# A chunked state-space scan feeding a bilinear feed-forward: from four-block waves to a hand-ordered pipeline over blocks of 128 tokens

## The chip, the cores and the metric

One core of one Trainium2 chip. The metric is the device time of one execution in microseconds (us). TensorE, the matrix engine, appears as PE in the profile and its weight loads as PEld; VectorE is DVE, ScalarE is ACT, GpSimd is POOL, and SyncE, which here only issues transfers, is SP. PSUM is the accumulator memory that TensorE writes and DVE and ACT read; both kernels lay it out in banks of 512 float32 per partition. A matmul can be given a strip of 32 rows of TensorE's 128x128 array (row-tiled), of 32 columns (column-tiled), or of both; `tile_position` names the strip, and the profile prints its shape with a star, as `32*128`, `128*32` or `32*32`. The rest use the whole array (`128*128`).

A run more than 1.5% above the fastest of its kernel counts as slow and is left out of every ratio here; medians are of all runs.

## The reference

```python
# x: (4, 8, 768, 32)   a: (4, 8, 768)   B, C: (4, 8, 768, 16);   chunk = 32
for c in range(nc):
    ...
    cum = np.cumsum(la, axis=-1)                              # la = log a
    L = np.exp(cum[:, :, :, None] - cum[:, :, None, :]) * causal
    M = np.einsum('bhin,bhjn->bhij', Cc, Bc) * L
    y_intra = np.einsum('bhij,bhjd->bhid', M, xc)
    y_inter = np.einsum('bhin,bhnd->bhid', Cc, state) * np.exp(cum)[..., None]
    y[:, :, sl] = y_intra + y_inter
    state = decay_full[..., None, None] * state + np.sum(Bx, axis=2)
x = y.transpose(0, 2, 1, 3).reshape(3072, 256)
out = (x @ w_a) * (x @ w_b) @ w_out                           # 256 -> 1536 -> 256
```

Both kernels take chunks of 128 tokens instead of 32, which gives the same result: 6 blocks for each of 4 sequences, so 24 blocks, each with 8 heads of 32 channels and 16 states. The scan of a sequence is serial from block to block; the feed-forward of a block needs only that block's scan.

## The kernel before

The feed-forward works on groups of 512 tokens, four blocks. A group is put into a list of pieces when its four blocks have been scanned, and three pieces follow each later scan. The framework's scheduler may reorder what is written here.

```python
for b in range(nb):
    for blk in range(NBLK):
        emit_scaling(b, blk)                       # six DVE operations: BCm, Bd, Cd, CmE, CmO, X16
        ...
        # five transposes on TensorE: BCm, CmE, CmO, Cd, and Cd shifted by one head
        # scores: four row-tiled matmuls; mask by four DVE operations
        for u in range(2):
            for hh in range(4):                    # y_intra, column-tiled
                nc.tensor.matmul(py[32*g : 32*g+32, 0:128], X16[:, 32*h : 32*h+32], T1r[...], ...,
                                 tile_position=(0, 32 * g))
            for hh in range(4):                    # y_inter, one 16-row tile for each head
                nc.tensor.matmul(py[32*g : 32*g+32, 0:128], states16[blk][32*m : 32*m+16, ...], rhs_ci, ...,
                                 tile_position=(32 * m, 32 * g))
        ...
        if (_gb + 1) % 4 == 0 and ...:
            ffn_enqueue((_gb + 1) // 4 - 1)
        ffn_emit(3)
```

The feed-forward's matmuls stream 512 columns each; the output has one accumulator (`bufs=1`), so each of the four output groups of 128 tokens waits until the one before it has been copied out.

```python
for f in range(2):
    nc.tensor.matmul(a_ps, Wa[:, f, k*128 : (k+1)*128], X2T[:, f, j*NTOKT : (j+1)*NTOKT], ...)
...
nc.scalar.activation(out=a_sb, in_=a_ps, func=AF.Identity, scale=HSCALE)
nc.vector.scalar_tensor_tensor(out=hk, in0=b_ps, scalar=1.0, op0=ALU.mult, in1=a_sb, op1=ALU.mult)
...
pFO = ctx.enter_context(tc.tile_pool(name="pFO", bufs=1, space=bass.MemoryType.PSUM))
```

The head loads eight constants before the decays `a`, then takes their log and three cumulative sums for each of the six blocks, with three different triangular matrices (18 float32 matmuls).

## Time and profile before

| | before |
|---|---|
| time, median of 3 runs | 203.91 us (203.80 to 205.24) |
| span of the profiled run | 203.1 us |
| busy share PE, DVE, ACT, POOL | 87%, 56%, 44%, 11% |
| first feed-forward matmul | 41.88 us |
| last projection ends | near 192.4 us |

Three stretches are worth separating: up to the first feed-forward matmul, from there to the end of the last projection, and the rest. This is the view of the kernel before by stretch. Its columns are the stretch, its length, TensorE's busy time (and instructions), the granted clock, the share of the DMA engines, and GB/s.

```profile
0.00:41.88 41.88, 24.39 (x178) 1.00 1.01 137
41.88:192.40 150.52, 145.96 (x1200) 0.98 0.25 42
192.40:203.10 10.70, 5.48 (x44) 0.98 0.14 49
```

In the long middle stretch TensorE is idle for only 150.5 - 146.0 = 4.6 us. More speed there has to come from less TensorE work; the first and last stretch have waits to remove. Two rows of the table of groups show work that the change takes away or moves: the y_inter matmuls with 16 rows, and the scaling's cast of x, which leaves DVE. The columns are the shapes, the count, then busy us and the mean ns of one.

```profile
L400 PE MATMUL pyy<-BCT,st 16*32 16x128 f16 x96 | 11.9, 236 | 0.0
...
L225 DVE CAST x_all<-xf_all 128x256 f16<-128x256 f32 x24 | 7.0, 294 | 16.3 <-DMA xf_all<-in_x_dram 16.3
```

### The profile page before, as it was taken

The numbers are of one execution on the slowest core, as the hardware profiler recorded it, in microseconds if no ns is written. First come the engines' busy times: TensorE is split into PE (matmuls) and PEld (weight loads), VectorE is DVE, ScalarE is ACT, GpSimd is POOL, SyncE is SP. The second block draws the span as 40 slices with busy tenths as digits, with TensorE's granted clock in tenths as the row PEclk, the third lists the DMA queues.
The fourth block names the chain that finished last, engine by engine and source line by source line (L and its number), as shares of the span: only waits on it lengthen the run. The fifth ranks groups of instructions, "written<-read, shape, count | busy, mean of one in ns | idle before, by whom it ended". The sixth has DMA issues, their size and how long they took to land.

```text
span 203.1 us, 3886 instructions
## 1 busy us (share of the span) xinstructions
PE 175.8 (87%) x1418; PEld 94.5 (47%) x1418; DVE 113.4 (56%) x320; ACT 88.7 (44%) x226; POOL 21.9 (11%) x79
## 2 busy tenths in 40 slices
PE   0007989999999999999999998999989999899962
PEld 0007864433446444465434564344744346534442
DVE  6002148668897869988486422866225673236710
ACT  2013033535653456634456424565436564435511
POOL 5000202211011110011100111101111011100000
PEclk9999999999999889999999999999999999969999
DMA  5999998998899860001000010000110000200011
GB/s 75 211 222 159 113 112 98 110 111 106 104 114 127 102 129 31 0 26 60 21 0 0 17 65 31 2 0 3 52 52 3 0 0 29 77 0 2 3 52 52
DMA packets 81363, 12.53 MB, mean 62 GB/s; under 512 B 75648, under 2 KB 80800, under 8 KB 81344
## 3 DMA queue, kind: packets, MB, share of 16 engines
q1 hardware_dynamic: 79248, 9.93, 32.6%
q0 software_dynamic: 2096, 2.36, 7.2%
q8 instruction: 11, 0.18, 0.4%
q14 instruction: 8, 0.07, 0.1%
HBM read 11.50 MB, written 3.15 MB: 72 GB/s over the span
## 4 chain that ended last, share of the span: by engine, by line
PE 75%; ACT 7%; SPq 5%; DMA 4%; DVE 4%; issue 3%; ACTq 0%
PE a_ps L255 18%; PE o_ps L284 16%; PE b_ps L264 15%; PE pyy L381 8%; PE pa_m L357 6%; DMA xf_all<-in_x_dram 4%; PE pyy L400 4%; SPq L234 2%; ACT a_sb L273 2%; ACT o_sb L293 2%; DVE t1u L367 2%; PE pd L169 2%; PE q0a L329 2%; PE q1a L341 1%; PE pcum L169 1%
## 5 line engine op out<-in xcount | busy, mean ns | idle before, releaser
L275 DVE SCALAR_TENSOR_TENSOR hk<-b_ps,a_sb 128x512 f16<-128x512 f32 x72 | 49.8, 691 | 30.7 <-ACT a_sb L273 23.4
L273 ACT ACTIVATE a_sb<-a_ps 128x512 f32<-128x512 f32 x72 | 42.8, 599 | 26.1 <-PE a_ps L255 23.8
L367 DVE TENSOR_TENSOR t1u<-pa_m,caus_sb 128x256 f16<-128x256 f32 x96 | 35.7, 417 | 27.3 <-PE pa_m L357 27.1
L255 PE MATMUL a_ps<-x2t,Wa 128*128 128x512 f16 x144 | 47.3, 396 | 0.7 <-DVE hk L275 0.3
L264 PE MATMUL b_ps<-x2t,Wb 128*128 128x512 f16 x144 | 45.8, 393 | 0.0
L284 PE MATMUL o_ps<-Wo,hk 128*128 128x256 f16 x288 | 40.4, 273 | 2.1 <-ACT o_sb L293 1.5
L284 PEld LDWEIGHTS <-hk 128*128 128x128 f16 x288 | 26.0, 97 | 10.0 <-issue 3.2
L413 ACT CAST x2t<-pyy 128x128 f16<-128x128 f32 x48 | 12.7, 266 | 35.6 <-PE pyy L400 34.7
L381 PE MATMUL pyy<-t1u,x_all 128*32 128x128 f16 x192 | 21.7, 238 | 1.7 <-DVE t1u L367 0.4
L429 POOL TENSOR_TENSOR st<-st,CdBS 128x64 f32<-128x64 f32 x24 | 7.3, 304 | 135.5 <-ACT CdBS L351 135.5
L264 PEld LDWEIGHTS <-Wb 128*128 128x128 f16 x144 | 13.4, 98 | 16.0 <-issue 1.9
L381 PEld LDWEIGHTS <-x_all 128*32 128x32 f16 x192 | 9.6, 94 | 21.4 <-issue 17.5
L255 PEld LDWEIGHTS <-Wa 128*128 128x128 f16 x144 | 13.0, 100 | 14.0 <-issue 6.5
L357 PE MATMUL pa_m<-BCT 32*128 32x256 f16 x96 | 16.6, 294 | 2.7 <-ACT BCT L334 2.4
L293 ACT ACTIVATE o_sb<-o_ps 128x256 f32<-128x256 f32 x24 | 9.2, 383 | 21.4 <-PE o_ps L284 18.5
L225 DVE CAST x_all<-xf_all 128x256 f16<-128x256 f32 x24 | 7.0, 294 | 16.3 <-DMA xf_all<-in_x_dram 16.3
L132 PE MATMUL p_lat<-ident,la 32*128 32x32 f32 x12 | 2.8, 398 | 15.0 <-ACT la L128 15.0
L334 ACT CAST BCT<-q0a 128x384 f16<-128x384 f32 x24 | 11.5, 478 | 4.9 <-PE q0a L332 4.7
L400 PE MATMUL pyy<-BCT,st 16*32 16x128 f16 x96 | 11.9, 236 | 0.0
L400 PE MATMUL pyy<-CdBS,st 16*32 16x128 f16 x96 | 11.6, 235 | 0.0
L357 PEld LDWEIGHTS <-BCT 32*128 32x128 f16 x96 | 5.2, 92 | 10.1 <-issue 4.4
L132 PEld LDWEIGHTS p_lat<-ident,la 32*128 32x128 f32 x12 | 2.6, 324 | 15.0 <-ACT la L128 15.0
(53 smaller groups left out, 147.6 us busy)
## 6 DMA issues: line engine op xcount, KB each, us to landing
xf_all<-in_x_dram SPq DMA_DIRECT2D x24, 128.0 KB, 3.3
out_dram<-o_sb SPq DMA_DIRECT2D x24, 128.0 KB, 1.7
bn_all<-in_B_dram SPq DMA_DIRECT2D x24, 64.0 KB, 3.1
cn_all<-in_C_dram SPq DMA_DIRECT2D x24, 64.0 KB, 3.0
Wa<-in_moe_w_a_dram POOLq DMA_DIRECT2D x1, 768.0 KB, 7.3
Wb<-in_moe_w_b_dram POOLq DMA_DIRECT2D x1, 768.0 KB, 10.8
Wo<-in_moe_w_out_dram POOLq DMA_DIRECT2D x1, 768.0 KB, 14.9
p_sb<-p SPq DMA_DIRECT2D x2, 64.0 KB, 8.1
```

The source lines that it names most:

```text
L255: nc.tensor.matmul(a_ps, Wa[:, f, k * 128 : (k + 1) * 128], X2T[:, f, j * NTOKT : (j + 1) * NTOKT], start=(f == 0), stop=(f == 1), skip_gr ...
L264: nc.tensor.matmul(b_ps, Wb[:, f, k * 128 : (k + 1) * 128], X2T[:, f, j * NTOKT : (j + 1) * NTOKT], start=(f == 0), stop=(f == 1), skip_gr ...
L273: nc.scalar.activation(out=a_sb, in_=a_ps, func=AF.Identity, scale=HSCALE)
L275: nc.vector.scalar_tensor_tensor(out=hk, in0=b_ps, scalar=1.0, op0=ALU.mult, in1=a_sb, op1=ALU.mult)
L284: nc.tensor.matmul(o_ps, hks[k][:, st * 128 : (st + 1) * 128], Wo[:, k, :], start=(k == 0), stop=(k == NK - 1), skip_group_check=True,)
L293: nc.scalar.activation(out=o_sb, in_=o_ps, func=AF.Identity, scale=1.0 / HSCALE)
L334: nc.scalar.copy(BCT[:, 0:384], q0a[:, 0:384])
L357: nc.tensor.matmul(pa_m, BCT[32 * m : 32 * m + 32, 0:128], BCT[32 * m : 32 * m + 32, 128:384], start=True, stop=True, skip_group_check=Tru ...
L367: nc.vector.tensor_tensor(out=T1s[m // 2][:, (m % 2) * 256 : (m % 2) * 256 + 256], in0=pa_tiles[m], in1=caus_sb[:, 0:256], op=ALU.mult,)
L381: nc.tensor.matmul(py[32 * g : 32 * g + 32, 0:128], X16[:, 32 * h : 32 * h + 32], T1r[:, hh * 128 : hh * 128 + 128], start=True, stop=Fals ...
L400: nc.tensor.matmul(py[32 * g : 32 * g + 32, 0:128], states16[blk][32 * m : 32 * m + 16, (b * 2 + par) * 32 : (b * 2 + par) * 32 + 32,], rh ...
L413: nc.scalar.copy(X2T[:, u, b * S + blk * 128 : b * S + blk * 128 + 128], pys[u][:, 0:128],)
```

## The change

The intent is to feed TensorE without gaps from early on:

1. **Order by hand.** The scheduler is switched off. Turn t holds the scan of block t, the projections of block t-1, and the output of block t-2.
2. **Blocks of 128 tokens in the feed-forward too**, four 128-column products side by side in one PSUM bank, so it starts after the first block and not after four.
3. **Mid-block decay factors.** One pair of factors, exp(+c) for C and exp(-c) for B, with c counted from the middle of the block, serves scores, y_inter and the carry. The state is carried as it stands at the middle of the next block; a single factor `G` for each block and head takes it from middle to middle.
4. **Block-diagonal state.** The eight 16x32 states are spread into one 128x256 matrix with zeros elsewhere, so y_inter is two full matmuls and not eight small ones.
5. **PSUM.** Transposes, scan output, carry and scores share one tile `SC` of four banks; four further banks rotate for the feed-forward.
6. **Head.** The decays are loaded first, the weights come in seven pieces, TensorE runs 40 dummy matmuls, and the scaling moves from DVE to POOL.

The core of the diff, with cuts:

```diff
-    NTOKT = 512
-    ident = const.tile([128, 128], f16)
-    nc.sync.dma_start(ident, id128_t.ap())
-    ...                                              # seven more constants, then a
+    nc.sync.dma_start(a_sb, a.rearrange("b h s -> (b h) s"))
+    nc.scalar.dma_start(c32, p32_t.ap())
+    nc.scalar.dma_start(c16, p16_t.ap())
+    ...
+    psf = ctx.enter_context(tc.tile_pool(name="psf", bufs=4, space=PSUM))
+    SC = ps4.tile([128, 4, 512], f32, name="SC")
+    TT = SC[:, 0, :].bitcast(f16)
+    PY = SC[:, 1, :]
+    DS = SC[:, 2, :]
+    M3 = SC[:, 3, :]
+    ctx.enter_context(tc.manual_schedule())
+    ...
+    nc.tensor.matmul(cums, P63, laT, ...)            # one cumulative sum from mid-block, all blocks
+    nc.scalar.activation(out=fB, in_=cums, func=AF.Exp, scale=-1.0)
+    nc.scalar.activation(out=fC, in_=cums, func=AF.Exp)
+    ...
+    def pv(t):
+        if blk > 0:
+            for u in range(2):
+                nc.tensor.matmul(PY[:, u*128 : u*128+128], s["Sbd"][:, u*128 : u*128+128], s["BCT"][:, 256:384], ...)
+        ...                                          # y_intra into PY, carry into DS, both column-tiled
+        nc.scalar.activation(out=X2T[:, t], in_=PY[:, 0:256]..., func=AF.Copy, scale=YS / XS)
+        nc.vector.scalar_tensor_tensor(out=U32[:, b, blk + 1, :], in0=DS[:, 0:D], scalar=g, op0=ALU.mult,
+                                       in1=gU[:, b, blk, :], op1=ALU.add)
+        nc.gpsimd.tensor_tensor(out=Sbd..., in0=U32[:, b, blk + 1, :]...broadcast..., in1=maskbd..., op=ALU.mult)
+    ...
-            ffn_emit(3)
-    ffn_emit(1000)
+    for t in range(NT + 2):
+        scores(t); mask(t, 0)                        # (abridged)
+        scale(t + 1, ...); load(t + 3)
+        ffn_unit(t - 1, 0); mask(t, 1)
+        ffn_unit(t - 1, 1); ffn_unit(t - 1, 2)
+        pv(t)
+        transposes(t + 1)
+        ffn_out(t - 2)
```

## The prediction

> **What bounds the kernel now.** I read the page first, for who is busy and when.
>
> ```profile
> PE 175.8 (87%) x1418; PEld 94.5 (47%) x1418; DVE 113.4 (56%) x320; ACT 88.7 (44%) x226; POOL 21.9 (11%) x79
> ...
> PE   0007989999999999999999998999989999899962
> ...
> PEclk9999999999999889999999999999999999969999
> DMA  5999998998899860001000010000110000200011
> ```
>
> TensorE is full from slice 4 to 38 (a slice is 5.08 us); DVE and ACT have half the span free, and DMA, full for the first third, is idle after it. So there are three parts: a head without matmuls, a long body bound by TensorE, a short tail. The chain that ended last, in order of time, gives their limits:
>
> ```profile
> 10.58 8.52 DMA xf_all<-in_x_dram
> ...
> 29.89 0.44 PE pa_m L357 x2
> 33.25 0.80 PE pa_m L357 x4
> 36.54 0.80 PE pa_m L357 x4
> 39.83 0.80 PE pa_m L357 x4
> 41.95 0.52 PE a_ps L255
> ...
> 95.93 0.67 PE pa_m L357 x4
> ...
> 122.76 0.67 PE pa_m L357 x4
> ...
> 149.95 0.67 PE pa_m L357 x4
> ```
>
> Head: four blocks are scanned alone, 3.3 us each, and only at 41.95 does the feed-forward begin. Body: the same four-block pattern returns after 26.83 and 27.19 us, so 6.75 us a block. The tail I read in the timeline: the last feed-forward ends near 192.5, four output groups follow one by one at 2 us (one accumulator), and the span ends at 203.1.
>
> Next, in the timeline of TensorE, what one matmul really costs, because a busy TensorE is not one at its peak: I read the spacing of starts.
>
> ```profile
> 35.16 0.31 PE L330 MATMUL q0a<-ident,cme 128*128 128x128 f16 x1
> 35.27 0.31 PE L331 MATMUL q0a<-ident,cmo 128*128 128x128 f16 x1
> ...
> 94.92 0.22 PE L330 MATMUL q0a<-ident,cme 128*128 128x128 f16 x1
> 94.98 0.22 PE L331 MATMUL q0a<-ident,cmo 128*128 128x128 f16 x1
> 95.04 0.22 PE L332 MATMUL q0a<-ident,cd_all 128*128 128x128 f16 x1
> 95.09 0.22 PE L337 MATMUL q1a<-ident,cd_all 128*128 128x128 f16 x1
> ```
>
> The same 128-column matmul, each with its own weight load, is 110 ns from the next at 35 us and 55 ns at 95 us. The clock was half until about 45 us, which the page's clock row (9 there) does not show. Twelve 256-column output matmuls take 1.47 us, so 109 ns each; two 512-column ones 0.43 us, 215 each. Useful floor per block at full clock: 12 x 0.215 (288 / 24 matmuls) = 2.6 for the two projections and 12 x 0.109 = 1.3 for the output, 3.9 us. Of the 6.75, 2.85 us is scan.
>
> **What the Trainium skill says.** "TensorE: Matmul & The Clock Gate", section Back-to-back issue gap: N / 2.4 + 2.5 ns warm, but about 81 ns for a stream of load-and-multiply pairs at N = 128. This trace agrees with the first (55, 109, 215) over five pairs and has no long stream to test the second. The same page, Part 1: The HAM clock gate: half clock until about 3.4 us of sustained work; here 110 against 55 ns, and the full rate came 3.4 us after the dense matmuls of 41.9 us began. "TensorEngine Tiling (Array Packing)", Key Properties: changing the tiling mode drains the array; here seven output matmuls take 0.87 us to the next, column-tiled, instruction where 0.76 is due, so 0.1 us a change. "GPSIMD Engine Reference", 3.1 Elementwise — side-by-side cycle accounting: about 2.6 cycles (1.2 GHz) an element for two inputs; a 128x64 one takes 293 to 304 ns here, so about 0.16 us fixed plus 2.2 ns an element.
>
> **The change part by part.** Feed-forward per block of 128 tokens: 48 matmuls of 128 columns in place of 12 of 512: 48 x 0.0555 = 2.66 us, nothing gained, and four times the weight loads. Output: the same 12, 1.31 us, but spread through the body, so the tail of four serial groups falls to one. Scan: the block-diagonal state replaces eight 16-row matmuls by two full ones; one factor pair serves both scores and carry, so transposes go from five to three and the separate decay matmuls of the head, 36 of 400 ns and paired passes, become one. TensorE's scan work: 3 transposes 0.17; scores 0.11 + two mode changes 0.21; state 0.11, change 0.1, eight column-tiled in two rounds 0.13, eight 32-column ones 0.07, change hidden by the wait below: 0.9 us. Sum 4.87 us of TensorE work per block against 6.75.
>
> Other engines per block: ACT 3 x 0.599 (L273) + 0.478 (L334) + 2 x 0.383 (L293's size) = 3.04. DVE 3 x 0.691 (L275), two masks of 512 elements at the same 0.69, a 32-element update of some 0.19: 3.65. POOL, estimated with the 2.6 cycles: 2 x 0.3 + 0.44 + 0.72 + about 0.65 = 2.4. None is the bound.
>
> But the new kernel puts transposes, scores, outputs and carry in one PSUM tile of four banks, and the compiled program's list of waits shows what that makes: the next block's transposes wait for the DVE state update of this block, the update waits for the ACT eviction of the scan output, though they touch different banks. From the end E of this block's last carry matmul: 0.25 to the eviction (as from the last output matmul to its eviction), 0.38, 0.03, update 0.19, 0.06 back to TensorE (as hk to o_ps): 0.9 us in which TensorE can do nothing, because the output matmuls stand behind the transposes. With F the start of a block's feed-forward: mask 0.15 to 0.84, first product waits for its ACT copy, 1.33 to 2.02, second mask to 2.66, so TensorE starts the state part at 2.72, E is 3.14, products end near 3.9, the update near 4.08, transposes at 4.14, output to 5.62, scores to 5.94. One block in six has no update: 5.65. Mean 5.9 us, of which some 1.0 is stall.
>
> Head: the 96 KB of decays are now first in the queue instead of after eight constants (landing near 3 us, an estimate from the 1.5 to 1.9 us of the small loads; 12.1 us of waiting before), then six transposes, log, cumulative matmul, exponentials near 8, scaling and transposes 9 to 10, a 32x768 log 0.84 and reduce 0.93 ahead of the masks on DVE, masks to 13.4, state part, first eviction and update 15, block 1's scores 16.3, feed-forward 16.6. It begins cold: 3.4 us at half clock, ends near 20.9, and with the waits block 2's feed-forward starts near 24. Body: 21 periods x 5.9 = 124, to 148. End: state and output 4.5, last feed-forward 2.7, two outputs 2.7, to 158; eviction, store and end as before, 203.1 - 199.7 = 3.4, to 161. The measured time exceeds the span by 0.8 (203.9 - 203.1). Sum 162; I add 3 for unlisted waits (the old body carried about 1 us a block over its own floors) and a few for late weights: **165 us**. Of the 39 saved, about 18 are the head, 15 to 18 the body from block 2 on, the rest the tail.
>
> **The rivals.** (1) The stream of 128-column pairs is bound by weight loads at 81 ns: 48 x 0.026 = 1.2 us a block on the path: 29 more, about 190. For it: one load lasts 97 ns in the table. Against: five pairs ran at 55 with loads overlapping. (2) The whole-tile wait is hidden, because the matmul queue or my latencies are off: 5.0 us a block, 145. Against it: TensorE runs in order. (3) DMA binds: the input loads are 3072 packets a block, 32.6% x 203.1 / 24 = 2.75 us of all engines a block, under 5.9; but in the head they compete with 7.2% x 203.1 = 14.6 us of weights, asked for only from 7 us on, in seven pieces. If the third pieces or the output weights are late, 3 to 6 us more, once. (4) The clock falls to half again through the 1 us pauses: then up to 2.7 us a block. Against: the old body had pauses and stayed at 55 ns; its half-clock relapse at 70 us followed a scan-heavy stretch without dense matmuls, which the new turns avoid.
>
> **Range and chances.** Period 5.5 to 6.4 moves 11 us either way, the head 4: 154 to 178, prediction 165. All but rival 4 at full size leave a gain far over 2%: faster 0.97, same 0.02, slower 0.01.
>
> **What would show it.** Feed-forward starts 55 ns apart in the timeline (81 for rival 1); a period of 5.9 us; before each block's first transpose an idle of about 1 us with the DVE state update as releaser, some 20 us in all; TensorE busy share still over 75%; first feed-forward near 17 us; ACT and DVE under 70%. Wrong would be: no such idle (rival 2), transposes or scores waiting for POOL (its estimate too low), weight DMAs ending the first waits by more than 5 us, or 110 ns spacing in the body.

## The result, and the profile after

| | before | after |
|---|---|---|
| median of the runs made together | 204.57 us | 159.57 us |
| ratio, 95% interval | | 0.7767 (0.7714 to 0.7821) |
| span of the profiled run | 203.1 us | 157.8 us |
| TensorE busy / idle | 175.8 / 27.3 us | 130.4 / 27.4 us |

A ratio is the mean time of one kernel's fast runs over that of the other's fast runs of the same rounds, so it is not quite the ratio of the medians quoted. The output was correct, as it was in every experiment below. One of the four runs after, 162.81 us, was slow and is left out of the ratio.

The page of the changed kernel, busy shares and two of the rows by slices (a slice is now 3.95 us):

```profile
PE 130.4 (83%) x2146; PEld 115.5 (73%) x2146; DVE 82.8 (53%) x147; ACT 75.1 (48%) x150; POOL 65.8 (42%) x141
...
PE   7936967897897797797897797797888788788990
...
PEclk9999999999999999999999999999999999999997
```

The digits tell the story before any query does: TensorE is at work from the first slice, but in the body only about every third slice has a 9, with 7 or 8 between, where the kernel before had 9 in nearly all of them. Something small and regular is missing in each block. The same view by stretch, for the kernel after, cut at its own first feed-forward matmul and its own last projection:

```profile
0.00:14.16 14.16, 9.10 (x88) 1.00 1.04 152
14.16:151.30 137.14, 118.53 (x2039) 1.00 0.50 74
151.30:157.80 6.50, 2.77 (x27) 0.87 0.12 40
```

(The clock column reads 1.00 in the head, but matmuls of 128 columns start 106 ns apart there up to 19.2 us and 56 ns apart later; the spacing shows the half clock, the column does not.) The head is 41.88 - 14.16 = 27.7 us shorter, the middle 150.5 - 137.1 = 13.4, the tail 10.7 - 6.5 = 4.2: together the 45.3 us between the spans. The middle now holds more of the scan than before, 23 blocks and not 20, and still TensorE's busy time in it fell by 146.0 - 118.5 = 27.4 us. Only half of that came out as time, because its idle time rose from 4.6 to 137.1 - 118.5 = 18.6 us. What it waits for is in the list of waits (engine, line, who releases it: us in all, times, longest):

```profile
PE SC L173 <- DVE U L254: 13.9, 16, 0.9
...
PE SC L173 <- DVE U L252: 3.5, 4, 0.9
...
PE SC L173 <- ACT X2T L246: 1.5, 3, 0.5
```

All 23 waits are of one line, the first transpose of the next block, and the sum is 13.9 + 3.5 + 1.5 = 18.9 us. One of them, 0.78 us, lies in the head; the other 22 make 18.1 of the 18.6 us of the middle. One period of the timeline (start, us, engine, line, operation, in brackets the idle time before it and its releaser):

```profile
85.75 0.62 PE L279 MATMUL aps<-X2T,Wa 128*128 128x128 f16 x8
86.21 0.61 PE L279 MATMUL bps<-X2T,Wb 128*128 128x128 f16 x8
...
88.44 0.28 PE L212 MATMUL SC<-bct,sbd 128*128 128x128 f16 x2
...
88.77 0.22 PE L237 MATMUL SC<-x,Bz 128*32 128x32 f16 x8
...
89.06 0.38 ACT L246 ACTIVATE X2T<-SC 128x256 f16<-128x256 f32 x1 [0.22 <-PE SC L237]
89.54 0.25 DVE L254 SCALAR_TENSOR_TENSOR U<-SC,G,gU 128x32 f32<-128x32 f32 x1
89.85 0.27 PE L173 MATMUL SC<-c,Bz 128*128 128x128 f16 x2 [0.86 <-DVE U L254]
```

Six projection groups of eight take from 85.75 to 88.44, 2.69 us for 48 matmuls, so 56 ns each. The carry's last matmul ends at 88.77 + 0.22 = 88.99; then one engine after another takes its turn, ACT from 89.06, DVE from 89.54, and TensorE starts at 89.85. The DVE update reads the carry's bank; the transposes write another one, and their inputs have long been there. They share only the tile `SC`.

Two more rows, which the experiments use. The columns are as before, and the last is the idle time ahead of the group:

```profile
L173 PE MATMUL SC<-c,Bz 128*128 128x128 f16 x48 | 6.8, 223 | 18.8 <-DVE U L254 13.9
L167 POOL TENSOR_SCALAR x<-xn 128x256 f16<-128x256 f32 x24 | 20.3, 847 | 4.2 <-DMA xn<-in_x_dram 2.3
```

The first says the same 18.8 us a second way. The second is the cast of x on POOL, 847 ns where DVE took 294 before; POOL is 42% busy and can afford it in the body.

### The profile page after: what moved, and what is told of

Its sections match the earlier page's. It is cut to its first block, busy times and chain, and to the rows that moved or that the text cites. A ratio compares the mean times of both kernels' runs of the same rounds, so it can differ in the third digit from the quotient of the medians.

```text
span 157.8 us, 5256 instructions
## 1 busy us (share of the span) xinstructions
PE 130.4 (83%) x2146; PEld 115.5 (73%) x2146; DVE 82.8 (53%) x147; ACT 75.1 (48%) x150; POOL 65.8 (42%) x141
## 3 DMA queue, kind: packets, MB, share of 16 engines
q0 software_dynamic: 3184, 2.36, 9.7%
## 4 chain that ended last, share of the span: by engine, by line
PE 65%; DVE 17%; ACT 11%; issue 5%; ACTq 0%; DVEq 0%
PE ops L297 20%; PE aps L279 20%; DVE hk L289 12%; PE bps L279 12%; ACT asb L288 8%; PE SC L173 4%; PE SC L186 3%; PE wps L128 3%; DVE U L254 3%; ACT X2T L246 1%; PE SC L176 1%; ACT bct L178 1%; DVE t L199 1%; PE SC L224 1%; DVE hs L325 1%
## 5 line engine op out<-in xcount | busy, mean ns | idle before, releaser
L199 DVE TENSOR_TENSOR t<-SC,c 128x512 f16<-128x512 f32 x48 | 32.8, 686 | 45.3 <-PE SC L186 39.8
L288 ACT COPY asb<-aps 128x512 f32<-128x512 f32 x72 | 42.2, 585 | 28.2 <-PE aps L279 28.0
L289 DVE TENSOR_TENSOR hk<-bps,asb 128x512 f16<-128x512 f32 x72 | 47.5, 685 | 14.7 <-ACT asb L288 12.1
L279 PE MATMUL aps<-X2T,Wa 128*128 128x128 f16 x576 | 45.5, 224 | 0.0
L279 PE MATMUL bps<-X2T,Wb 128*128 128x128 f16 x576 | 45.3, 223 | 0.0
L258 POOL TENSOR_TENSOR sbd<-U,c 128x256 f16<-128x256 f32 x20 | 13.3, 666 | 66.9 <-DVE U L254 46.1
L279 PEld LDWEIGHTS <-Wa 128*128 128x128 f16 x576 | 35.4, 100 | 2.5 <-issue 0.2
L279 PEld LDWEIGHTS <-Wb 128*128 128x128 f16 x576 | 36.4, 100 | 0.0
L297 PE MATMUL ops<-Wo,hk 128*128 128x256 f16 x288 | 35.2, 273 | 0.0
L173 PE MATMUL SC<-c,Bz 128*128 128x128 f16 x48 | 6.8, 223 | 18.8 <-DVE U L254 13.9
L167 POOL TENSOR_SCALAR x<-xn 128x256 f16<-128x256 f32 x24 | 20.3, 847 | 4.2 <-DMA xn<-in_x_dram 2.3
```

Of the source, the lines that this page charges most:

```text
L167: eng_c.tensor_scalar(X16, Xn.rearrange("p h d -> p (h d)"), XS, None, ALU.mult)
L173: nc.tensor.transpose(TT[:, e * 128 : (e + 1) * 128], Bz[:, s["z"], e].rearrange("p h n -> p (h n)"), ident)
L199: nc.vector.tensor_tensor(out=T1[:, 4 * half : 4 * half + 4, :].rearrange("p (m e) q -> p m (e q)", e=2), in0=SC[:, 2 * half : 2 * half + ...
L258: nc.gpsimd.tensor_tensor(out=Sbd.rearrange("p (h d) -> p h d", d=D), in0=U32[:, b, blk + 1, :].unsqueeze(1).broadcast_to((128, H, D)), in ...
L279: nc.tensor.matmul(ps[:, kk * Q : (kk + 1) * Q], W[:, f, k * 128 : (k + 1) * 128], X2T[:, t, f, :], start=(f == 0), stop=(f == 1), skip_gr ...
L288: nc.scalar.copy(a16, a_ps)
```

## The experiments

All ratios are to the kernel before, run in the same rounds on the same chip. Medians are of the runs of each kernel.

### 1. Two tiles in place of one

If the 18.9 us come from the shared tile, then splitting `SC` into two tiles of two banks, with the four uses placed so that the next transposes share a tile with nothing late, should remove them without moving one instruction. (Lines of three hunks, joined.)

```diff
-    SC = ps4.tile([128, 4, 512], f32, name="SC")
-    TT = SC[:, 0, :].bitcast(f16)
-    PY = SC[:, 1, :]
-    DS = SC[:, 2, :]
-    M3 = SC[:, 3, :]
+    S01 = ps4.tile([128, 2, 512], f32, name="S01")
+    S23 = ps4.tile([128, 2, 512], f32, name="S23")
+    TT = S01[:, 0, :].bitcast(f16)
+    PY = S23[:, 1, :]
+    DS = S23[:, 0, :]
+    M3 = S01[:, 1, :]
 ...
-                    SC[:, m, e * 128 : (e + 1) * 128],
+                    (S01, S23)[m // 2][:, m % 2, e * 128 : (e + 1) * 128],
 ...
-            in0=SC[:, 2 * half : 2 * half + 2, 0:256],
+            in0=(S01, S23)[half][:, :, 0:256],
```

> The one four-bank PSUM tile is cut in two tiles of two banks, transposes in the first (bank 0), outputs and carry in the second (banks 3 and 2); operations, order and sizes stay. Theory (the tracker's whole-tile wait is the idle before each block's transposes): the waits of transposes for the state update vanish, 16 x 0.87 + 4 x 0.88 + 3 x 0.5 = 18.9 us less; period 5.89 to about 5.03 us, time about 141 us. Rival (the transposes' results would be waited for anyway, by the scores through the ACT copy, or ACT and DVE are simply too slow): period stays near 5.9, 157 to 160 us; the idle then stands before the scores.

Measured: 141.09 us (140.34 to 141.47), ratio 0.6877 (0.6821 to 0.6934). The period of a block (from its first projection to the next block's) fell from 5.89 to 4.97 us. In its timeline the transposes follow the carry at once and the output follows them:

```profile
88.55 0.21 PE L238 MATMUL S<-x,Bz 128*32 128x32 f16 x8
88.70 0.29 PE L174 MATMUL S<-c,Bz 128*128 128x128 f16 x2
...
88.88 1.47 PE L298 MATMUL ops<-Wo,hk 128*128 128x256 f16 x12
...
89.33 0.25 DVE L255 SCALAR_TENSOR_TENSOR U<-S,G,gU 128x32 f32<-128x32 f32 x1
```

The DVE update starts at 89.33, after the transposes have started at 88.70: they never depended on it. Operations and order are the same. `PY` and `M3` have changed places among the banks, but experiment 2, which leaves every use in the bank that it has in the change, shows that the bank is not what counts. So the shared tile made the stall, and its price, 159.57 - 141.09 = 18.5 us, is about the 18.9 us of the list of waits.

### 2. Two tiles, but the scan output beside the transposes

The rival reading of experiment 1 is that any two tiles help. Here `PY` goes into the tile of the transposes, so they should wait for ACT's copy of it but no longer for DVE. The lines are set against experiment 1's kernel; each use is again in the bank that it has in the change.

```diff
-    PY = S23[:, 1, :]
-    M3 = S01[:, 1, :]
+    PY = S01[:, 1, :]
+    M3 = S23[:, 1, :]
```

> The same cut, but the scan output stays in the transposes' tile (bank 1) and only the carry (bank 2) lies in the other. Theory: the transposes still wait for the ACT eviction of the scan output, not for the DVE update after it, so the idle falls from 0.87 to about 0.50 us a block, as in the four places of the changed kernel where no update follows: 20 x 0.37 = 7.4 us less, about 152 us, period about 5.5. Rival (any wait of the transposes counts the same, or banks matter rather than tiles): equal to the other cut (141) or to no cut (159).

Measured: 152.10 us (151.72 to 152.46), ratio 0.7419 (0.7351 to 0.7487). The waits of its profile name the new releaser:

```profile
PE S L174 <- ACT X2T L247: 9.5, 21, 0.5
```

So the tile decides, not the number of tiles: the wait is for whatever was last read from the same tile. The stall also splits here into its parts: 0.45 us a block (9.5 / 21) up to the end of the eviction, the rest of the 0.86 for the update.

### 3. Output first, then the transposes, one tile

If the stall is only a matter of order, TensorE could do the output of block t-2 while ACT and DVE finish.

```diff
-        if t + 1 < NT:
-            transposes(t + 1)
         if 2 <= t:
             ffn_out(t - 2)
+        if t + 1 < NT:
+            transposes(t + 1)
```

> One tile as in the changed kernel, but the output matmuls of block t-2 stand before the transposes of t+1 instead of after. Theory: 1.31 us of output matmuls fill the 0.87 us wait, but nothing is left between transposes and scores, so the scores wait 0.3 + 0.48 + 0.06 us for the ACT copy of the transposes: the wait moves, period 5.8 to 5.9, time 157 to 160. Rival (the wait alone is the cost and any filler gains it): about 141 us.

Measured: 158.57 us (156.75 to 159.05), ratio 0.7718 (0.7644 to 0.7792), not told apart from the change itself. The wait has moved to the scores, which need ACT's copy of the transposes:

```profile
86.47 0.29 PE L186 MATMUL SC<-bct 32*128 32x128 f16 x8 [0.68 <-ACT bct L178]
```

The output's 1.3 us can hide one of two waits of this loop, the one ahead of the transposes or the one behind them, and this order only swaps which.

### 4. Output in two parts: seven matmuls ahead, five behind

Then splitting it should hide both. This order is what the scheduler found by itself in experiment 5, which was run first.

```diff
-    def ffn_out(t):
+    def ffn_out(t, part):
-        for k in range(NK):
+        for k in range(0, 7) if part == 0 else range(7, NK):
 ...
+        if 2 <= t:
+            ffn_out(t - 2, 0)
         if t + 1 < NT:
             transposes(t + 1)
         if 2 <= t:
-            ffn_out(t - 2)
+            ffn_out(t - 2, 1)
```

> The changed kernel, one PSUM tile, hand order, but seven of the twelve output matmuls before the next block's transposes and five after, as the framework's scheduler had chosen. Theory (each of the two waits, 0.87 us for the update and 0.85 us for the copy of the transposes, is covered by what stands beside it): 0.76 us cover the first but for 0.1, 0.55 us the second but for 0.25, period 5.25 as the scheduler's, 23 x 0.62 = 14 us less, about 145. Rival (the scheduler's body was shorter for another reason): 155 to 160.

Measured: 145.87 us (145.59 to 146.49), ratio 0.7108 (0.7072 to 0.7145), and a period of 5.22 us. No idle time is printed on these lines of its timeline:

```profile
87.29 0.94 PE L299 MATMUL ops<-Wo,hk 128*128 128x256 f16 x7
88.23 0.27 PE L173 MATMUL SC<-c,Bz 128*128 128x128 f16 x2
...
88.40 0.71 PE L299 MATMUL ops<-Wo,hk 128*128 128x256 f16 x5
```

With the tile left whole, order alone recovers 13.7 of the 18.5 us. It does not reach experiment 1: the period is 5.22 against 4.97. The spacing of the lines says why, although they print no idle time: seven matmuls at 0.109 us are 0.76, but the transposes start 0.94 after the first of them. That is where the handover of 0.86 us behind the carry ends (the carry's last record ends at 87.36), so a rest of it, 0.18 of the 0.25 us, still shows, hidden in the modelled end of a group.

### 5. The scheduler's order in place of the hand's

The change has two sides, the algorithm and the order. One line gives the order back to the scheduler.

```diff
-    ctx.enter_context(tc.manual_schedule())
```

> The changed kernel's operations with the hand order given up: the framework's scheduler orders each engine's instructions. Theory (order by turns is a good part of the gain, since TensorE runs in order and each stage needs the one before it from other engines): over 170 us. Rival (the gain is from fewer and earlier operations; any sane order will do): 155 to 165 us.

Measured: 157.14 us (fast runs 154.95 to 157.16), ratio 0.7629 (0.7542 to 0.7717). My theory that the hand order is worth more than 10 us fell as stated: the sum is about the same. But the two halves of it are not. In the body the scheduler is better, with the seven-and-five order and a period of 5.24 us. In the head it is worse:

```profile
25.01 0.55 POOL L157 TENSOR_TENSOR Bz<-bn,fB 128x64 f16<-128x64 f32 x2 [4.11 <-DMA bn<-in_B_dram]
...
28.33 0.67 POOL L257 TENSOR_TENSOR sbd<-U,c 128x256 f16<-128x256 f32 x1
...
29.05 0.39 PE L211 MATMUL SC<-bct,sbd 128*128 128x128 f16 x2 [6.49 <-POOL sbd L257]
```

The last line is the second block's state matmul, at 29.05 us; in the hand order it is at 19.26. It waits for POOL's spreading of the state (`sbd`), which is at 28.33 us here and at 13.94 in the hand order: the scheduler put it behind the scaling of later blocks, for whose inputs POOL stands waiting. Six of the seven weight transfers are also issued before the first scaling, and not two. Experiment 4 has almost this body with the hand's head, 145.87 us, so the scheduler's body gains 159.57 - 145.87 = 13.7 us and its head loses 157.14 - 145.87 = 11.3. A comparison of the two times alone would have read this as "order does not matter".

### 6. The scheduler's order with two tiles

With the stall taken away from both, only the head should tell the orders apart. It is experiment 1 without the same line.

> The two-tile kernel with the hand order given up. Theory (in the body any order that keeps TensorE fed gives 5.0 to 5.25 us a block, with or without the hand; the hand order is worth some 11 us in the head alone, where the scheduler lets block 1's state part wait for POOL until 29 us, as in the scheduler's one-tile run against the one with seven and five output matmuls, 157.1 against 145.9): 150 to 154 us, period 5.0 to 5.25. Rival (without the whole-tile waits the scheduler finds as good a head): 140 to 144.

Measured: 154.32 us (153.26 to 155.11), ratio 0.7552 (0.7483 to 0.7622), just above the 150 to 154 that I had expected. The body's period is 4.97 us (the same block mark at 42.23 and 47.20, and at 91.71 and 96.68), exactly that of the hand order; the second block's state matmul stands at 31.89 us after 8.95 us of waiting for POOL. In the hand order (experiment 12) that matmul is at 18.55 us, so 31.89 - 18.55 = 13.3 of the 151.9 - 138.4 = 13.5 us between the two profiled spans are already there. The gain of the hand order is the head's, with next to nothing left for the body. The two kernels were not run in the same rounds; the medians differ by 13.8 us.

### 7. The block-diagonal state undone

The same state, multiplied as eight 32x32 tiles and not as two full matrices. The halves of the output were put in two banks here. (Cuts are marked by `...`; some `start` flags change too.)

```diff
-            for u in range(2):
+            for h in range(H):
                 nc.tensor.matmul(
-                    PY[:, u * 128 : u * 128 + 128],
-                    s["Sbd"][:, u * 128 : u * 128 + 128],
-                    s["BCT"][:, 256:384],
+                    PY[32 * g : 32 * g + 32, u, 0:128],
+                    s["Sbd"][32 * m : 32 * m + 32, 32 * h : 32 * h + 32],
+                    s["BCT"][32 * m : 32 * m + 32, 256:384],
 ...
+                    tile_position=(32 * m, 32 * g),
```

> One part of the change undone: the block-diagonal state product (two full matmuls a block) is done as eight 32x32-tiled ones again, two of them into a second bank[...]. Theory (the block-diagonal form saves one change of tiling mode, and eight tiled ones take about as long as two full ones): 20 blocks x 0.05 to 0.12 us more, 160.5 to 162. Rival (the block-diagonal state is a main part of the gain of the scan): 165 us or more.

Measured: 161.31 us (160.14 to 162.22), ratio 0.7851 (0.7806 to 0.7895). That is 1.7 us over the change, with intervals that just overlap. The period, 5.96 against 5.89 us, gives the same size: 0.07 x 21 = 1.5 us. Its timeline shows where it lies. The eight small matmuls take 0.18 us up to the next instruction, the two full ones 0.20; but from the start of the last projection group to the state matmul it is 0.54 us and not 0.45. So the block-diagonal form as such is worth nothing here; what it saves is a change of tiling mode, which is the next experiment.

### 8. Two more mode changes a block

On experiment 1's kernel, each full state matmul is followed by its half of the column-tiled y_intra, so TensorE changes between whole-array and column-tiled mode twice more in each of 20 blocks. Not one instruction is added.

```diff
-        if blk > 0:
-            for u in range(2):
-                ...                                # both state matmuls
-        for u in range(2):
+        for u in range(2):
+            if blk > 0:
+                ...                                # state matmul u
             for g in range(4):
                 ...                                # four of y_intra
```

> The kernel with two PSUM tiles, with the same matmuls, but the two halves of the state part in turns: full state product, four column-tiled, full, four column-tiled. That is two more changes of tiling mode in each of 20 blocks, and no other work. Theory (a change costs TensorE about 0.1 us, and the kernel before has 288 of them against 96): 40 x 0.105 = 4.2 us more than the two-tile kernel, about 145.3; period 5.18 instead of 4.97. Rival (changes cost nothing much when the matmuls are independent): 141 to 142.

Measured: 145.38 us (144.13 to 145.67), ratio 0.7071 (0.7031 to 0.7110), so 4.9 us over the same kernel in the same rounds (experiment 12), and a period of 5.19 against 4.97 us. Its timeline:

```profile
85.45 0.22 PE L212 MATMUL S<-bct,sbd 128*128 128x128 f16 x1
85.60 0.24 PE L222 MATMUL S<-t,x 128*32 128x128 f16 x4
85.77 0.23 PE L212 MATMUL S<-bct,sbd 128*128 128x128 f16 x1
```

From a full matmul to the tiled ones behind it is 0.15 us, where two full ones follow each other in 0.056. By the period, a change of mode costs (5.19 - 4.97) / 2 = 0.11 us. Counted on the timelines, the kernel before changes mode some 12 times a block, about 290 in all (49 in the four blocks from 95.93 us on), and the kernel after 4 times, some 96 in all. Times 0.11 that would be some 20 us, of the 27 us of TensorE time that the middle lost. This product is an estimate: the cost was measured in the new kernel, not on the old one's changes.

### 9. More dummy matmuls in the head

The first block's projections run at half clock, in spite of the change's own 40 dummy matmuls: from 14.16 us on, 48 of them take 5.1 us, 106 ns each, and only the second block's are at 56 ns. 33 more dummy matmuls in the gaps ahead of and around them should bring the full clock earlier.

```diff
     transposes(0)
+    warmup(5)
 ...
     G = big.tile([128, nb * NG], f32, name="G")
+    warmup(12)
 ...                                               # and 5, 6, 5 in turn 0
```

> 33 more dummy matmuls fill TensorE's idle places between 7.8 and 14 us. Theory (the half clock of block 0's feed-forward, 107 ns a matmul until about 19 us, comes of too little continuous work before it): it starts at the full clock, 48 x 0.05 = 2.4 us less, about 157. Rival (dummy matmuls on zeros do not raise the clock[...]): no change, 158.5 to 160.5, starts still 107 ns apart at 14 to 17 us.

Measured: 159.42 us (159.26 to 162.62, the last one slow), ratio 0.7788 (0.7735 to 0.7841): no gain, where I had expected 2.4 us. The clock did rise earlier, near 16.7 us and not near 19.2, but then the projections caught up with their weights:

```profile
17.65 0.62 PE L279 MATMUL aps<-X2T,Wa 128*128 128x128 f16 x8 [0.28 <-DMA Wa<-in_moe_w_a_dram]
18.85 0.62 PE L279 MATMUL bps<-X2T,Wb 128*128 128x128 f16 x8 [0.58 <-DMA Wb<-in_moe_w_b_dram]
```

The second block's projections began at 21.84 us where the change has 21.94. The half clock had been hiding the late weights. It also cannot be said that the dummies caused the early rise: experiment 1's kernel, with none of them, had the full clock near 16.7 us in one profile and near 17.2 in another.

### 10. The kernel before with its decays loaded first

One part of the change done alone on the old kernel: the load of `a` ahead of the constants.

```diff
     const = ctx.enter_context(tc.tile_pool(name="const", bufs=1))
+    a_sb0 = const.tile([32, S], f32, name="a_sb0")
+    nc.sync.dma_start(a_sb0, a.rearrange("b h s -> (b h) s"))
     ident = const.tile([128, 128], f16)
```

> The kernel before, with the load of the decays moved from behind the eight constants to the front of the queue; nothing else. Theory (the head waits for the decays' load, 12.1 us, and then for its own 36 fp32 matmuls): the log starts near 3 instead of 14 us, the scan some 8 to 10 us earlier than 27.9, time about 195 to 197. Rival (the head is bound by the DMA engines, full until 70 us, so that the inputs of the scan come no earlier): 202 to 205 us.

Measured: 201.94 us (fast runs from 200.07; one slow of 204.34), ratio 0.9805 (0.9731 to 0.9878), about 4 us less; both of the expected ranges missed it. The log of the decays moved from 14.08 to 2.86 us, 11.2 us, but its successors then wait for what stands behind it in the queue:

```profile
8.95 0.61 PE L169 MATMUL pcum<-laT,triu_sb 128*128 128x32 f32 x2 [2.43 <-DMA triu_sb<-triu]
```

The first feed-forward matmul came at 35.09 us, 6.8 earlier, and the middle stretch grew from 150.5 to 153.1 us, by 1.1 us of idle and 1.5 us of busy time on TensorE. Where in it these lie was not pursued.

### 11. A better head for the split kernel

An attempt at the best version: on experiment 1's kernel, earlier weights, the cast of the first block's x on DVE, the second block's scaling ahead of the output weights' transfer, and 27 more dummy matmuls. The diff is cut.

```diff
-    nc.gpsimd.tensor_copy(scr[:, 0:1], blk_in[0][0][:, 0, 0:1])
+    nc.gpsimd.tensor_copy(scr[:, 0:1], c32[:, 0:1])
 ...
-    for d, s_ in wq[0:2]:
+    for d, s_ in wq[0:3]:
-    scale(0, nc.vector, nc.gpsimd)
-    for d, s_ in wq[2:6]:
+    scale(0, nc.vector, nc.gpsimd, nc.vector)
+    for d, s_ in wq[3:6]:
         nc.gpsimd.dma_start(d, s_)
+    scale(1, nc.vector, nc.gpsimd)
     nc.gpsimd.dma_start(Wo, moe_w_out.rearrange("(k p) e -> p k e", p=128))
 ...                                               # warmup(5), (12), (5), (5); the scaling of turn 0 goes
```

> A try at the best: two PSUM tiles, dummy matmuls in the idle places up to block 0's feed-forward, and the weights asked for earlier (not after the first block's input but after the constants), with block 1's scaling before the output weights. Theory (the dummy matmuls gained nothing alone because the weights were then late by 0.86 us and the whole-tile waits followed): 1 to 3 us less than the two-tile kernel, 138 to 140. Rival (earlier weights take DMA time from the first inputs and give it back): 141 or more.

Measured: 142.85 us (141.86 to 143.52), ratio 0.6949 (0.6904 to 0.6994): 2.3 us slower than without it. The first block's projections began 1.2 us earlier (13.02 against 14.26), but the second block's state matmul had to wait:

```profile
20.02 0.29 PE L213 MATMUL S<-bct,sbd 128*128 128x128 f16 x2 [2.36 <-POOL sbd L259]
```

POOL's own timeline has the reason:

```profile
17.25 0.86 POOL L168 TENSOR_SCALAR x<-xn 128x256 f16<-128x256 f32 x1 [5.47 <-DMA cn<-in_C_dram]
...
19.29 0.68 POOL L259 TENSOR_TENSOR sbd<-U,c 128x256 f16<-128x256 f32 x1
```

It stands 5.5 us before the second block's cast, for an input transfer (the profile names that of C; the cast reads x), then casts, issues the output weights, and spreads the state only at 19.29, for which TensorE waits. The second block's projections then ran at half clock again from 22.38 to near 25 us. So the weights' gain was paid back by inputs that came later to POOL, which did its instructions in the order written.

### 12. The split kernel again

Experiment 1's kernel with five rounds, beside the two above, as their base and as the best version.

> The two-tile kernel once more, beside the two others: 140 to 142.

Measured: 140.51 us (140.14 to 141.21), ratio 0.6849 (0.6815 to 0.6884). It beats both kernels. By stretch it looks like this; the head and tail are those of the change, and the middle has 117.7 - 116.6 = 1.2 us of idle TensorE:

```profile
14.26:132.00 117.74, 116.57 (x2039) 1.00 0.59 87
```

## Why the prediction was right

The prediction was 165 us in a range of 154 to 178; 159.57 was measured. Step by step:

**The period held.** For a block with an update 5.94 us were worked out and 5.89 measured (a first transpose at 83.96, the next at 89.85). The chain inside it held too. Counted from the first projection at 85.75, the first mask came at 0.19 (worked out: 0.15), the first product at 1.33 (1.33), the state part at 2.69 (2.72), the carry's end at 3.24 (3.14), the transposes at 4.10 (4.14). The handover was worked out as 0.9 us and is 0.86, in part by terms that offset each other: the ACT eviction came sooner (0.07 us after the carry's end for 0.25) and the update was longer and later (0.10 + 0.25 for 0.03 + 0.19). Some of this is definition: the record's end of the carry is modelled, and the prediction counted it from the spacing of starts. One sum in the working is off, 2.02 + 0.69 is 2.71 and not 2.66; it did not matter, since the state part followed the projections without a wait.

**The stall was the tile's.** Some 20 us in all were predicted ahead of the transposes, released by the DVE update; 18.9 were found, and experiments 1 and 2 show that the shared tile makes them. The estimate of TensorE's own work, 4.87 us a block, is confirmed to 0.1 us by experiment 1: without the stall the period is 4.97.

**The rivals.** Rival 1, weight loads at 81 ns, is out: 56 ns over 48 pairs in a row. Rival 2, the wait hidden, is out in this kernel, and it was the right size: it said 145, and experiments 1 and 4, which do hide or remove it, gave 141 and 146. Rival 3, late weights, did not show in the change but stood right behind it (experiments 9 and 11). Rival 4, half clock in the pauses, did not show: the body has 56 ns throughout.

**What was mis-sized** are small terms of the sum. The head: the second block's projections (the prediction's block 2) began at 21.94, not 24, since the first block's began at 14.16 and not 16.6; at half clock those took until 19.2 us (106 ns each for all 48), longer than the 3.4 us allowed for, which gave part of it back. The periods: 21 of them took 144.17 - 21.94 = 122.2 us, 5.82 each, because a period with an update is 5.89 and not 5.94 and the few without one are shorter still; 124 were reckoned. The end from there to TensorE's last matmul took 9.9 us, as worked out (4.5 + 2.7 + 2.7). The 3 us added for unlisted waits and late weights were not needed. Against these, the last eviction and store took 3.7 us and not 3.4, and measured time exceeds span by 1.8 us and not 0.8. That 0.8 was a slip: it sets the median of three runs against the span of one of them. Wherever the record lists both for one run of the kernel before, the time exceeds the span by 1.9 to 2.1 us. So 165 - 2.1 - 1.8 - 3 + 0.3 + 1.0 = 159.4, which leaves 0.2, the rounding of the sum, to the 159.6 measured. POOL took 0.59 + 0.41 + 0.85 + 0.67 + 0.36 = 2.9 us a block where 2.4 was estimated; it had time to spare, so this cost nothing.

**The split of the gain** that the prediction gave (18 head, 15 to 18 body from the second block on, rest tail) is cut at other points than the stretches above, 27.7, 13.4 and 4.2, and cannot be checked against them number by number; the stretches say more about the head because the old head also scanned three blocks that the new middle holds.

**What stays open.** How the head's 27.7 us divide among its parts: some 13 us are what the hand order is worth against the scheduler's (experiment 6), some 4 us are what the early decays are worth in the old kernel (experiment 10), and the rest, the one cumulative sum and the start after one block, was not separated. And when the clock goes to full: 16.7, 17.2 or 19.2 us in profiles of nearly the same head.

## What to carry to other kernels

Give each PSUM use with its own lifetime its own tile: here four uses in one tile cost 18.5 of 159.6 us, and splitting the tile, without moving an instruction, gave them back. TensorE passed over no waiting matmul in these traces (the output matmuls stood behind the waiting transposes for 0.86 us a block), so look at what stands behind a waiting instruction, and put work from an older block on both sides of each handover to ACT or DVE. When a large reordering and its undoing give the same time, compare head and body apart before concluding that order does not matter: here 13.7 us one way and 11.3 the other cancelled.

## What the Trainium skill lacked or had wrong

- "TensorE: Matmul & The Clock Gate", section Back-to-back issue gap, gives about 81 ns as the sustained spacing of a stream of weight load and matmul pairs at N = 128. The runs show 56 ns for 48 pairs in a row, in every block of the changed kernel's body; the page's formula for a single gap, N / 2.4 + 2.5 (55.8 ns), fits here.
- The same page, Part 1: The HAM clock gate, puts the warm-up at about 3.4 us of sustained work and calls it variable from run to run. The variation is there: full rate near 16.7, 17.2 and 19.2 us in profiles whose projections all began near 14.2, so 2.5 to 5 us. It also gives about 3.4 us of idling for the way back; in experiment 11 half clock returned after a wait of 2.36 us and some 2 us of sparse work, with no single pause that long; which of the two brought it back no run here shows.
- "TensorEngine Tiling (Array Packing)", Key Properties, says that a change of tiling mode drains the array and gives no figure. Here it costs 0.11 us (experiment 8).
- "GPSIMD Engine Reference", section 4.1 Engine selection, calls one-input elementwise operations roughly line-rate on GpSimd. Here a one-input scaling of 128x256 from float32 to float16 took 847 ns there, more than the two-input product of the same size (666 ns), and a cast of that size on VectorE took 294 ns.
- No page that I used has it that the framework orders accesses by whole PSUM tile, across banks: 18.9 us of waiting in this kernel.
